# Moving 256 rows of an MLP's second weight to 40 partitions and five DMA engines

## The chip, the cores and the metric

The kernel runs on one core of a Trainium2 chip. The metric is the device time of one execution in microseconds, the median of several runs. The core has a tensor engine (PE, with a separate weight load, PEld), a vector engine (DVE), a scalar engine (ACT), a general engine (POOL), a sync engine (SP) that here only issues loads, and sixteen DMA engines that carry all of them.

## The reference

One decode step of a transformer block for two tokens (batch 2, one position each), width 576. The input is normalised, and an attention branch and an MLP branch are both added to it:

```python
xn = layernorm(x)                                   # x: 2 x 1 x 576
out = x + A(xn, k_cache, v_cache, wq, wo) + B(xn, w1, b1, w2, b2)

# A: 32 query heads over 16 key/value heads, last 2048 of 8192 positions
q = xn @ wq                                         # wq: 576 x 4096
p = softmax((q . k[:, :, 8192 - 2048:]) * 128 ** -0.5)
A = (p . v[:, :, 8192 - 2048:]) @ wo                # wo: 4096 x 576

# B: squared ReLU
h = max(xn @ w1 + b1, 0) ** 2                       # w1: 576 x 4608
B = h @ w2 + b2                                     # w2: 4608 x 576
```

All tensors are bfloat16. Nearly all of the work is reading: the page counts 53.62 MB read, of which the keys and values are 33.6 MB, and each of w1 and w2 5.3 MB.

## The kernel before, in words

**Attention.** The 32 pairs of batch and key/value head are done in NU = 8 units of four heads (`TH`). A unit's keys are one tile of 128 partitions x 8192 elements (16 KB per partition, 2 MB), its values another. `load_k` and `load_v` (L341 to L347) issue them from SP into a pool of six equal buffers, `kvpool`. `step(u)` (L363) transposes the keys of unit u on TensorE in eight groups (`transposes`, L232), multiplies them with the queries (`scores`, L245), and in between multiplies the values of unit u - 2 with their probabilities (`pv`, L281). `softmax` (L255) runs on DVE, POOL and ACT. After every second unit `wo_proj` (L297) projects four heads of both tokens onto the output.

**MLP.** `mlp_h_block(c)` (L316) multiplies the c-th block of 128 rows of w1 (the fifth block has the remaining 64) with the input and adds to a PSUM tile `hT_ps`; its output is transposed, with the hidden unit on the partition. The 4608 hidden units are cut into two halves of L1 = 2304 (S = 2), each half into FR = 18 columns: hidden unit s*2304 + p*18 + r sits on partition p in column s*18 + r. So there are NFC = 36 columns of 128 units, and 36 matmuls for each of five blocks. With the last block DVE adds b1 and squares (L327 to L333). `mlp_o` (L335) multiplies a column of h with the matching row of w2: for partition p and column r that is row s*2304 + p*18 + r, so a w2 tile has on partition p a run of consecutive rows of w2, r0 to r1, of 1152 bytes each. `issue_w2` (L126) loads such a piece into a buffer of the same pool as keys and values. The list of the pieces is

```python
W2P = [(0, 0, 9), (0, 9, 18), (1, 0, 9), (1, 9, 15), (1, 15, 18)]
```

that is, half, first row, end row: nine rows, nine, nine, six and three.

**Output.** `out_acc` (L211) does two matmuls of 288 columns for every row, the two halves of the width side by side in one PSUM tile `out_ps`. Everything adds to that tile: x itself and b2 at the start, the four projections of the attention, and the w2 rows. At the end DVE copies it (L414) and SP and ACT store a half each.

**Order.** The tile framework places each engine's instructions: it takes program order as priority and lets a later instruction go ahead when an earlier one isn't ready by its own reckoning. Waits and buffers are put in by it. In the profile SP issues in program order: queries' weights and the first keys, w1 between the first units, then values, wo and keys of the following units, and behind the last values (L407) the w2 pieces, each as soon as a buffer is free. POOL issues the two bias loads at the start (L146, L148).

Of the kernel before, what the change touches and what calls it, by code (L numbers as in the profile page):

```python
# [9 lines left out]
BF16 = mybir.dt.bfloat16  # L10
# [6 lines left out]
def kernel(  # L17
# [14 lines left out]
    nc = tc.nc  # L32
    P = 128
    B, Sq, D = A_x.shape
    _, Hkv, Sk, Dh = A_k_cache.shape
    Hq = A_wq.shape[1] // Dh
    F = B_w1.shape[1]
# [11 lines left out]
    NU = NQ * B  # L49
# [6 lines left out]
    S = P // REM  # L56
    KC = NFULL + 1
    NXN = NFULL + S
    LQ = (Hq * Dh) // S
    L1 = F // S  # L60
    FR = L1 // P
    NFC = S * FR
    OH = D // 2
    WR = NC * Dh // P
    DW = Dh // WR
# [2 lines left out]
    const = ctx.enter_context(tc.tile_pool(name="const", bufs=1))  # L68
# [12 lines left out]
    k_tiles, v_tiles, wq_tiles, w1_tiles, wo_tiles, w2_tiles = {}, {}, {}, {}, {}, {}  # L81
# [7 lines left out]
    def issue_kv(tiles, cache, u, name, parts=1):  # L89
        tl = kvpool.tile([P, UE], BF16, tag="kv", name=f"{name}_{u}")  # L90
        v = unit_view(cache, u)
        n = UE // parts
        tiles[u] = tl
        return [lambda i=i: nc.sync.dma_start(out=tl[:, i * n:(i + 1) * n], in_=v[:, :, i * n:(i + 1) * n])  # L94
                for i in range(parts)]
# [10 lines left out]
    def issue_wq(c):  # L106
        issue_w(wq_tiles, A_wq, c, "wq", Hq * Dh, LQ)
# [1 line left out]
    def issue_w1(c):  # L109
        issue_w(w1_tiles, B_w1, c, "w1", F, L1)  # L110

    def w_operands(tiles, c, col0, L, step=1):
        last = col0 + (P - 1) * step
        if c < NFULL:
            return tiles[c][:, col0:last + 1:step], c
        sg = col0 // L
        assert last // L == sg
        return tiles[c][:, col0 - sg * L:last - sg * L + 1:step], NFULL + sg

    def issue_wo(tq):  # L120
        tl = wopool.tile([P, WR, D], BF16, tag="wo_sb", name=f"wo_{tq}")
        n = NC * Dh
        nc.sync.dma_start(out=tl[:], in_=A_wo[tq * n:(tq + 1) * n, :].rearrange("(p r) n -> p r n", r=WR))
        wo_tiles[tq] = tl

    def issue_w2(s, r0, r1):  # L126
        tl = kvpool.tile([P, (r1 - r0) * D], BF16, tag="kv", name=f"w2_{s}_{r0}")
        rows = B_w2[s * L1:(s + 1) * L1, :].rearrange("(p r) n -> p (r n)", r=FR)
        nc.sync.dma_start(out=tl[:], in_=rows[:, r0 * D:r1 * D])
        w2_tiles[(s, r0)] = tl  # L130

    x_sb = const.tile([B, D], BF16, name="x_sb")
    nc.scalar.dma_start(out=x_sb[:], in_=x2d)
# [8 lines left out]
    k0[1]()  # L142
    for c in range(2, KC):
        issue_wq(c)
    b1_sb = const.tile([P, S, FR], BF16, name="b1_sb")
    nc.gpsimd.dma_start(out=b1_sb[:], in_=B_b1.rearrange("(s p r) -> p s r", s=S, p=P))  # L146
    b2_sb = const.tile([1, D], BF16, name="b2_sb")
    nc.gpsimd.dma_start(out=b2_sb[:], in_=B_b2.rearrange("(o n) -> o n", o=1))  # L148

# [39 lines left out]
    xnT = const.tile([P, NXN, B], BF16, name="xnT")  # L189
# [21 lines left out]
    def out_acc(lhsT, rhs_of, start=False, stop=False):  # L211
        for i in range(2):
            nc.tensor.matmul(out_ps[32 * i:32 * i + B, :], lhsT=lhsT, rhs=rhs_of(i * OH, (i + 1) * OH),  # L213
                             start=start, stop=stop, skip_group_check=True)
# [7 lines left out]
    def q_block(c):  # L222
        for h in range(Hq):
            lhsT, xc = w_operands(wq_tiles, c, h * Dh, LQ)
            nc.tensor.matmul(qT_ps[:, h, :], lhsT=lhsT, rhs=xnT[:, xc, :],  # L225
                             start=(c == 0 and h == 0), stop=(c == KC - 1), skip_group_check=True)
        if c == KC - 1:
            nc.vector.tensor_copy(out=qT_all[:].rearrange("p b h -> p h b"), in_=qT_ps[:])
# [52 lines left out]
    def pv(u, g):  # L281
        tq, b = divmod(u, B)
        if g == 0:
            oT_cur[u] = psum.tile([P, NC], F32, tag="misc", bufs=2, name=f"oT_ps_{u}")
        oT_ps = oT_cur[u]
        v_sb = v_tiles[u]
        for i in range(JG):
            j = g * JG + i
            nc.tensor.matmul(oT_ps[:], lhsT=v_sb[:, j * Dh:(j + 1) * Dh], rhs=pT_tiles[u][:, j, :],  # L289
                             start=(j == 0), stop=(j == NJ - 1))  # L290
        if g == NG - 1:
            if b == 0:
                oG_tiles[tq] = keep.tile([P, NC, B], BF16, tag="oG", name=f"oG_{tq}")
            nc.vector.tensor_tensor(out=oG_tiles[tq][:, :, b], in0=oT_ps[:], in1=rinv_tiles.pop(u)[:], op=ALU.mult)
            pT_tiles.pop(u)

    def wo_proj(tq):  # L297
        oG = oG_tiles.pop(tq)
        rr = work.tile([P, WR, NC * B], BF16, tag="rr", name=f"rr_{tq}")
        nc.vector.tensor_tensor(  # L300
            out=rr[:],
            in0=oG[:].rearrange("p h b -> p (h b)").unsqueeze(1).to_broadcast([P, WR, NC * B]),
            in1=rmask[:].unsqueeze(2).to_broadcast([P, WR, NC * B]), op=ALU.mult)
        wps = psum.tile([P, WR, B], F32, tag="misc", bufs=2, name=f"wps_{tq}")
        for h in range(NC):
            nc.tensor.matmul(wps[:], lhsT=sel[:, h, :, :].rearrange("p a c -> p (a c)"),
                             rhs=rr[:, :, h * B:(h + 1) * B], start=(h == 0), stop=(h == NC - 1))
        ws = work.tile([P, WR, B], BF16, tag="ws", name=f"ws_{tq}")
        nc.vector.tensor_copy(out=ws[:], in_=wps[:])  # L309
        wo_sb = wo_tiles.pop(tq)  # L310
        for r in range(WR):
            out_acc(ws[:, r, :], lambda a, z: wo_sb[:, r, a:z])

    mlp = {}

    def mlp_h_block(c):  # L316
        if c == 0:
            mlp["ps"] = psum.tile([P, NFC, B], F32, tag="misc", bufs=2, name="hT_ps")
        hT_ps = mlp["ps"]
        for s in range(S):  # L320
            for r in range(FR):
                lhsT, xc = w_operands(w1_tiles, c, s * L1 + r, L1, FR)
                nc.tensor.matmul(hT_ps[:, s * FR + r, :], lhsT=lhsT, rhs=xnT[:, xc, :],  # L323
                                 start=(c == 0 and s == 0 and r == 0), stop=(c == KC - 1), skip_group_check=True)
        if c == KC - 1:
            t1 = work.tile([P, NFC, B], F32, tag="t1", name="t1")
            nc.vector.tensor_tensor(out=t1[:], in0=hT_ps[:],  # L327
                                    in1=b1_sb[:].rearrange("p s r -> p (s r)").unsqueeze(2).to_broadcast([P, NFC, B]),
                                    op=ALU.add)
            hT_sb = const.tile([P, NFC, B], BF16, name="hT_sb")  # L330
            nc.vector.scalar_tensor_tensor(out=hT_sb[:], in0=t1[:], scalar=0.0, in1=t1[:],
                                           op0=ALU.max, op1=ALU.mult)
            mlp["h"] = hT_sb  # L333

    def mlp_o(s, r0, r1, last=False):  # L335
        w2_sb = w2_tiles.pop((s, r0))
        for r in range(r0, r1):
            o = (r - r0) * D
            out_acc(mlp["h"][:, s * FR + r, :], lambda a, z: w2_sb[:, o + a:o + z], stop=(last and r == r1 - 1))

    def load_k(u):  # L341
        for f in issue_kv(k_tiles, A_k_cache, u, "k"):
            f()

    def load_v(u):
        for f in issue_kv(v_tiles, A_v_cache, u, "v"):
            f()  # L347

    W2P = [(0, 0, 9), (0, 9, 18), (1, 0, 9), (1, 9, 15), (1, 15, 18)]

    load_k(1)
    issue_w1(0)
    issue_w1(1)
    load_v(0)
    load_k(2)
    for c in range(2, KC):
        issue_w1(c)
    load_v(1)
    issue_wo(0)
    load_k(3)  # L360
    nxt = {0: [], 1: [], 2: [lambda: load_v(2), lambda: load_k(4)]}

    def step(u, extra=()):  # L363
        for g in range(NG + 2):
            if g < NG:
                transposes(u, g)
            if u >= 1 and 1 <= g <= NG:
                if u >= 2:
                    pv(u - 2, g - 1)
            if g >= 2:  # L370
                scores(u, g - 2)
        softmax(u)
# [15 lines left out]
    for u in range(2, NU + 2):  # L388
        if u < NU:
            step(u)  # L390
        else:
            for g in range(NG):
                pv(u - 2, g)
        if u == 2:
            for c in range(2, KC):
                mlp_h_block(c)
        if u - 2 >= 1 and (u - 2) % B == B - 1:
            wo_proj((u - 2) // B)
        if u < NU:
            load_v(u)  # L400
            if u % B == 0:
                issue_wo(u // B)
            if u + 2 < NU:
                load_k(u + 2)
        if u >= NU - 1:
            pass
        if u == NU - 1:  # L407
            for w in W2P:
                issue_w2(*w)
    for i, w in enumerate(W2P):  # L410
        mlp_o(*w, last=(i == len(W2P) - 1))

# [34 lines left out]
```

## Time and profile before

| what | us |
|---|---|
| median of 3 runs | 137.40 (137.31 to 137.52) |
| the profiled execution's own time | 137.42 |
| its span, first to last instruction | 135.6 |
| PE busy | 102.5 (76%) |
| DVE busy | 53.9 (40%) |
| ACT busy | 43.0 (32%) |
| POOL busy | 10.0 (7%) |
| mean granted TensorE clock | 0.759 of full |
| moved by DMA | 53.90 MB, mean 397 GB/s |

The page of the profile gives, over the span, each engine's busy time, a row of forty slices with the busy share in tenths, the DMA queues with packets and bytes (q1 is SP's, q10 ACT's, q0 POOL's, q8 and q14 carry instructions), and the chain of work that ended last, followed back from the end. A line such as "start, length, PE out_ps L213 x6" is six matmuls of line 213 that write the tile out_ps. A query for stretches of time gives the engines' busy time, the granted TensorE clock and the mean busy share of the sixteen DMA engines in each. Behind these views lie the records of single DMA packets (queue, start, length, size, not the engine) and of the times at which a load's up to sixteen parts reported their landing.

### The profile page before, as it was taken

The numbers are of one execution on the slowest core, as the hardware profiler recorded it, in microseconds if no ns is written. First come the engines' busy times: TensorE is split into PE (matmuls) and PEld (weight loads), VectorE is DVE, ScalarE is ACT, GpSimd is POOL, SyncE is SP. The second block draws the span as 40 slices with busy tenths as digits, with TensorE's granted clock in tenths as the row PEclk, the third lists the DMA queues.
The fourth block names the chain that finished last, engine by engine and source line by source line (L and its number), as shares of the span: only waits on it lengthen the run. The fifth ranks groups of instructions, "written<-read, shape, count | busy, mean of one in ns | idle before, by whom it ended". The sixth has DMA issues, their size and how long they took to land.

```text
span 135.6 us, 4461 instructions
## 1 busy us (share of the span) xinstructions
PE 102.5 (76%) x2054; PEld 91.9 (68%) x2054; DVE 53.9 (40%) x124; ACT 43.0 (32%) x47; POOL 10.0 (7%) x31
## 2 busy tenths in 40 slices
PE   1049947599968999879943993999399599768961
PEld 0039947589968999839933993688399479664530
DVE  7502421574352325422653446355634645660001
ACT  6705550165012521004701550272155127110000
POOL 6400000110110001100011001101100110110000
PEclk9999985569855685556985698698559959955599
DMA  5999999999999999999999999999999999999940
GB/s 112 418 419 418 428 442 402 420 429 440 430 393 430 438 411 409 444 425 396 440 440 406 445 420 425 404 443 423 425 430 413 430 415 426 422 410 417 393 166 1
DMA packets 5278, 53.90 MB, mean 397 GB/s; under 512 B 630, under 2 KB 652, under 8 KB 1164
## 3 DMA queue, kind: packets, MB, share of 16 engines
q1 hardware_dynamic: 5188, 53.61, 94.7%
q8 instruction: 16, 0.26, 0.8%
q0 software_dynamic: 64, 0.01, 0.0%
q14 instruction: 2, 0.02, 0.0%
q10 hardware_dynamic: 8, 0.00, 0.0%
HBM read 53.62 MB, written 0.00 MB: 395 GB/s over the span
## 4 chain that ended last, share of the span: by engine, by line
DMA 55%; PE 35%; DVE 3%; issue 2%; POOL 1%; ACT 1%; SPq 1%; POOLq 0%; ACTq 0%
DMA k<-in_A_k_cache_dram 41%; PE kT_ps L237 18%; DMA w<-in_B_w_dram 10%; PE hT_ps L323 5%; DMA b_sb<-in_B_b_dram 4%; PE sc_ps L252 4%; PE out_ps L213 4%; PE oT_ps L289 3%; PE qT_ps L225 1%; ACT kT L240 1%; POOL b_sb L146 1%; DVE l L271 1%; DVE sub L266 1%; SPq L94 0%; DVE fin_sb L414 0%
## 5 line engine op out<-in xcount | busy, mean ns | idle before, releaser
L237 PE MATMUL kT_ps<-ident,k 128*128 128x128 bf16 x512 | 47.3, 260 | 9.9 <-DMA k<-in_A_k_cache_dram 9.9
L237 PEld LDWEIGHTS <-k 128*128 128x128 bf16 x512 | 39.6, 119 | 11.8 <-DMA k<-in_A_k_cache_dram 10.7
L240 ACT COPY kT<-kT_ps 128x1024 bf16<-128x1024 bf16 x32 | 32.3, 1012 | 40.1 <-PE kT_ps L237 40.0
L242 DVE COPY kT<-kT_ps 128x1024 bf16<-128x1024 bf16 x32 | 22.0, 690 | 33.4 <-PE kT_ps L237 33.4
L252 PE MATMUL sc_ps<-qT_all,kT 128*128 128x8 bf16 x512 | 21.6, 168 | 1.6 <-ACT kT L240 0.8
L252 PEld LDWEIGHTS <-kT 128*128 128x128 bf16 x512 | 19.1, 100 | 2.6 <-ACT kT L240 1.2
L289 PE MATMUL oT_ps<-pT,v 128*128 128x8 bf16 x512 | 15.5, 167 | 1.9 <-issue 1.4
L269 ACT ACTIVATE pT<-sub 128x512 bf16<-128x512 f32 x8 | 5.0, 630 | 35.1 <-DVE sub L266 35.1
L289 PEld LDWEIGHTS <-v 128*128 128x128 bf16 x512 | 14.4, 99 | 2.1 <-issue 1.6
L271 DVE TENSOR_REDUCE l<-pT 128x8 f32<-128x512 bf16 x8 | 8.5, 1066 | 4.2 <-ACT pT L269 4.2
L213 PE MATMUL out_ps<-wo,ws 128*2 128x288 bf16 x64 | 8.3, 438 | 2.4 <-DVE ws L309 2.4
L323 PE MATMUL hT_ps<-xnT,w 128*128 128x2 bf16 x144 | 9.8, 201 | 0.0
L323 PEld LDWEIGHTS <-w 128*128 128x128 bf16 x144 | 9.4, 165 | 0.0
L258 DVE TENSOR_REDUCE m<-sc_ps 128x8 f32<-128x512 f32 x8 | 5.5, 692 | 9.7 <-PE sc_ps L252 9.7
L262 POOL PARTITION_ALL_REDUCE gmax<-m x8 | 2.9, 364 | 84.8 <-DVE m L260 84.8
L213 PE MATMUL out_ps<-w,hT_sb 128*2 128x288 bf16 x72 | 6.9, 353 | 1.3 <-DMA w<-in_B_w_dram 1.3
L213 PEld LDWEIGHTS <-ws 128*2 128x2 bf16 x64 | 3.5, 115 | 5.4 <-DVE ws L309 2.8
L213 PEld LDWEIGHTS <-hT_sb 128*2 128x2 bf16 x72 | 3.8, 103 | 4.3 <-issue 1.9
L266 DVE TENSOR_TENSOR sub<-sc_ps,gm 128x512 f32<-128x512 f32 x8 | 5.5, 692 | 0.3
L225 PE MATMUL qT_ps<-xnT,wq 128*128 128x2 bf16 x128 | 4.0, 165 | 2.2 <-DMA wq<-in_A_wq_dram 1.9
L225 PEld LDWEIGHTS <-wq 128*128 128x128 bf16 x128 | 3.9, 103 | 2.2 <-DMA wq<-in_A_wq_dram 2.0
L273 POOL PARTITION_ALL_REDUCE lsum<-l x8 | 3.2, 398 | 24.5 <-DVE l L271 24.5
(58 smaller groups left out, 35.1 us busy)
## 6 DMA issues: line engine op xcount, KB each, us to landing
v<-in_A_v_cache_dram SPq DMA_DIRECT2D x8, 2048.0 KB, 28.4
k<-in_A_k_cache_dram SPq DMA_DIRECT2D x7, 2048.0 KB, 29.4
w<-in_B_w_dram SPq DMA_DIRECT2D x4, 1152.0 KB, 17.7
wo<-in_A_wo_dram SPq DMA_DIRECT2D x4, 1152.0 KB, 27.4
wq<-in_A_wq_dram SPq DMA_DIRECT2D x4, 1024.0 KB, 6.9
w<-in_B_w_dram SPq DMA_DIRECT2D x3, 1296.0 KB, 22.7
k<-in_A_k_cache_dram SPq DMA_DIRECT2D x2, 1024.0 KB, 9.1
w<-in_B_w_dram SPq DMA_DIRECT2D x1, 864.0 KB, 15.7
```

What stands on the lines that cost most here:

```text
L213: nc.tensor.matmul(out_ps[32 * i:32 * i + B, :], lhsT=lhsT, rhs=rhs_of(i * OH, (i + 1) * OH), start=start, stop=stop, skip_group_check=True)
L225: nc.tensor.matmul(qT_ps[:, h, :], lhsT=lhsT, rhs=xnT[:, xc, :], start=(c == 0 and h == 0), stop=(c == KC - 1), skip_group_check=True)
L237: nc.tensor.transpose(out=kT_ps[:, i * P:(i + 1) * P], in_=k_sb[:, j * Dh:(j + 1) * Dh], identity=ident[:])
L240: nc.scalar.copy(out=kT[:], in_=kT_ps[:])
L242: nc.vector.tensor_copy(out=kT[:], in_=kT_ps[:])
L252: nc.tensor.matmul(sc_ps[:, g * JG + i, :], lhsT=kT[:, i * P:(i + 1) * P], rhs=qT_all[:, b, tq * NC:(tq + 1) * NC], start=True, stop=True)
L258: nc.vector.tensor_reduce(out=m1[:], in_=sc_ps[:].rearrange("p j c -> p c j"), axis=AX.X, op=ALU.max)
L266: nc.vector.tensor_tensor(out=sub[:], in0=sc_ps[:], in1=gm2[:].unsqueeze(1).to_broadcast([P, NJ, NC]), op=ALU.subtract)
L269: nc.scalar.activation(out=pT[:], in_=sub[:], func=ACT.Exp, scale=scale)
L271: nc.vector.tensor_reduce(out=l1[:], in_=pT[:].rearrange("p j c -> p c j"), axis=AX.X, op=ALU.add)
L289: nc.tensor.matmul(oT_ps[:], lhsT=v_sb[:, j * Dh:(j + 1) * Dh], rhs=pT_tiles[u][:, j, :], start=(j == 0), stop=(j == NJ - 1))
L323: nc.tensor.matmul(hT_ps[:, s * FR + r, :], lhsT=lhsT, rhs=xnT[:, xc, :], start=(c == 0 and s == 0 and r == 0), stop=(c == KC - 1), skip_g ...
```

## The change

256 of the 4608 rows of w2, the last ones, leave the 128-partition pieces. The second half keeps FT = 16 columns of 128 units (2048 units) in place of 18. Of the other 256 units 240 are laid on 40 partitions with six columns (XR = 6, XP = 40), so partition p holds six consecutive rows of w2, and the last 16 on 16 partitions with one column. The 240 rows are loaded by eight DMAs of five partitions each (partitions i, i+8, i+16, i+24 and i+32), one behind each of `load_v(1)`, `load_k(3)`, `load_v(2)`, `load_k(4)` and so on; the 16 rows follow the eighth. They have tiles of their own. `mlp_x`, new, does their seven columns after `pv` of unit 6. There are now 41 columns in h; `hT_ps` is set to zero by DVE first, and b1 by POOL, since some columns don't fill all partitions; b1 comes in four loads in place of one. The w2 pieces become nine, nine, nine, four, two and one rows. Two unused statements go.

```diff
+    XR, XP = 6, 40
+    FT = (L1 - XR * XP) // P
+    FX = L1 - FT * P
+    XQ = FX - XR * XP
+    FX0 = L1 + FT * P
+    CH = [(r, FR, P) for r in range(FR)] + [(L1 + r, FT, P) for r in range(FT)]
+    CH += [(FX0 + r, XR, XP) for r in range(XR)] + [(FX0 + XR * XP, 1, XQ)]
+    NFC = len(CH)
...
     def issue_w2(s, r0, r1):
+        nr = FT if s else FR
...
+        rows = B_w2[s * L1:s * L1 + nr * P, :].rearrange("(p r) n -> p (r n)", r=nr)
...
+    x_parts = list(range(8))
+
+    def issue_w2x():
+        if x_parts:
+            i = x_parts.pop(0)
+            rows = B_w2[FX0:FX0 + XR * XP, :].rearrange("(e i r) n -> i e (r n)", i=8, r=XR)
+            nc.sync.dma_start(out=w2x_sb[i:XP - 8 + i + 1:8, :], in_=rows[i])
+            if not x_parts:
+                nc.sync.dma_start(out=w2y_sb[:], in_=B_w2[FX0 + XR * XP:F, :])
...
-    b1_sb = const.tile([P, S, FR], BF16, name="b1_sb")
-    nc.gpsimd.dma_start(out=b1_sb[:], in_=B_b1.rearrange("(s p r) -> p s r", s=S, p=P))
+    b1_sb = const.tile([P, NFC], BF16, name="b1_sb")
+    nc.gpsimd.memset(b1_sb[:], 0.0)
+    o = 0
+    for f0, n, m in ((0, FR, P), (L1, FT, P), (FX0, XR, XP), (FX0 + XR * XP, 1, XQ)):
+        nc.gpsimd.dma_start(out=b1_sb[0:m, o:o + n], in_=B_b1[f0:f0 + n * m].rearrange("(p r) -> p r", r=n))
+        o += n
...
             mlp["ps"] = psum.tile([P, NFC, B], F32, tag="misc", bufs=2, name="hT_ps")
+            nc.vector.memset(mlp["ps"][:], 0.0)
...
+        for i, (f0, step, m) in enumerate(CH):
+            lhsT, xc = w_operands(w1_tiles, c, f0, L1, step, m)
+            nc.tensor.matmul(hT_ps[0:m, i, :], lhsT=lhsT, rhs=xnT[:, xc, :],
+                             start=(c == 0 and i == 0), stop=(c == KC - 1), skip_group_check=True)
...
+    def mlp_x():
+        for i, (f0, step, m) in enumerate(CH[FR + FT:]):
+            w = w2x_sb[0:m, i * D:(i + 1) * D] if m == XP else w2y_sb[:]
+            out_acc(mlp["h"][0:m, FR + FT + i, :], lambda a, z: w[:, a:z])
...
     def load_k(u):
...
+        if u >= 3:
+            issue_w2x()
...
     def load_v(u):
...
+        if u >= 1:
+            issue_w2x()
...
-    W2P = [(0, 0, 9), (0, 9, 18), (1, 0, 9), (1, 9, 15), (1, 15, 18)]
+    W2P = [(0, 0, 9), (0, 9, 18), (1, 0, 9), (1, 9, 13), (1, 13, 15), (1, 15, 16)]
...
+        if u == NU:
+            mlp_x()
```

More of the change, by code (lines that the diff above doesn't have):

```diff
@@ L61 @@
     FR = L1 // P
-    NFC = S * FR
+    XR, XP = 6, 40
[6 more added lines that the diff above has]
+    NFC = len(CH)
     OH = D // 2
@@ L110, in issue_w1, with w_operands @@
         issue_w(w1_tiles, B_w1, c, "w1", F, L1)
-    def w_operands(tiles, c, col0, L, step=1):
-        last = col0 + (P - 1) * step
+    def w_operands(tiles, c, col0, L, step=1, m=P):
+        last = col0 + (m - 1) * step
         if c < NFULL:
@@ L126, in issue_w2 @@
     def issue_w2(s, r0, r1):
+        nr = FT if s else FR
         tl = kvpool.tile([P, (r1 - r0) * D], BF16, tag="kv", name=f"w2_{s}_{r0}")
-        rows = B_w2[s * L1:(s + 1) * L1, :].rearrange("(p r) n -> p (r n)", r=FR)
+        rows = B_w2[s * L1:s * L1 + nr * P, :].rearrange("(p r) n -> p (r n)", r=nr)
         nc.sync.dma_start(out=tl[:], in_=rows[:, r0 * D:r1 * D])
         w2_tiles[(s, r0)] = tl
+    w2x_sb = const.tile([P, XR * D], BF16, name="w2x_sb")
+    w2y_sb = const.tile([XQ, D], BF16, name="w2y_sb")
+    x_parts = list(range(8))
[6 more added lines that the diff above has]
+                nc.sync.dma_start(out=w2y_sb[:], in_=B_w2[FX0 + XR * XP:F, :])
     x_sb = const.tile([B, D], BF16, name="x_sb")
@@ L318, in mlp_h_block @@
             mlp["ps"] = psum.tile([P, NFC, B], F32, tag="misc", bufs=2, name="hT_ps")
+            nc.vector.memset(mlp["ps"][:], 0.0)
         hT_ps = mlp["ps"]
[L320 to L324, printed above, removed]
+        for i, (f0, step, m) in enumerate(CH):
+            lhsT, xc = w_operands(w1_tiles, c, f0, L1, step, m)
+            nc.tensor.matmul(hT_ps[0:m, i, :], lhsT=lhsT, rhs=xnT[:, xc, :],
+                             start=(c == 0 and i == 0), stop=(c == KC - 1), skip_group_check=True)
         if c == KC - 1:
@@ L327, in mlp_h_block @@
             nc.vector.tensor_tensor(out=t1[:], in0=hT_ps[:],
-                                    in1=b1_sb[:].rearrange("p s r -> p (s r)").unsqueeze(2).to_broadcast([P, NFC, B]),
+                                    in1=b1_sb[:].unsqueeze(2).to_broadcast([P, NFC, B]),
                                     op=ALU.add)
@@ L360 @@
     load_k(3)
-    nxt = {0: [], 1: [], 2: [lambda: load_v(2), lambda: load_k(4)]}
     def step(u, extra=()):
@@ L404 @@
                 load_k(u + 2)
-        if u >= NU - 1:
-            pass
+        if u == NU:
+            mlp_x()
         if u == NU - 1:
```

## The prediction

> **What bounds the kernel now.** I read the page's summary first, then the chain that ended last, then the stretches of the last 14 us, and last the records of single DMA packets. The page:
>
> ```profile
> span 135.6 us, 4461 instructions
> DMA  5999999999999999999999999999999999999940
> q1 hardware_dynamic: 5188, 53.61, 94.7%
> q8 instruction: 16, 0.26, 0.8%
> ```
>
> The DMA engines are at 9 tenths from the second slice to the 38th; the loads (q1) fill 94.7% of sixteen engines' span. No other engine is above 76%. So time is bytes, and what follows the last byte. The end of the chain (start, length, what) shows the second part:
>
> ```profile
> 119.21 13.05 DMA w<-in_B_w_dram
> 132.26 0.04 issue
> 132.30 0.55 PE out_ps L213 x6
> 132.85 0.02 issue
> 132.87 0.45 DVE fin_sb L414
> ```
>
> The last piece of w2 lands at 132.26, its six matmuls (three rows, two halves each) take 0.55, then comes the copy-out. Now the stretches (PE, PEld, DVE, ACT, POOL busy; then granted clock, DMA share, GB/s):
>
> ```profile
> 118.14:121.55 3.41, 2.21 (x71) 2.08 (x72) 2.25 (x5) 0.63 (x1) 0.40 (x1) 0.50 1.01 421
> 121.55:124.97 3.42, 2.51 (x29) 1.41 (x29) 0.64 (x3) 0.00 (x0) 0.00 (x0) 0.50 0.99 405
> 124.97:128.38 3.41, 3.41 (x32) 1.86 (x30) 0.00 (x0) 0.00 (x0) 0.00 (x0) 0.50 0.99 409
> 128.38:129.20 0.82, 0.54 (x10) 0.26 (x8) 0.00 (x0) 0.00 (x0) 0.00 (x0) 1.00 0.69 279
> 129.20:131.20 2.00, 1.23 (x18) 0.75 (x18) 0.00 (x0) 0.00 (x0) 0.00 (x0) 1.00 0.50 191
> 131.20:132.30 1.10, 0.90 (x12) 0.52 (x12) 0.00 (x0) 0.00 (x0) 0.00 (x0) 1.00 0.22 85
> ```
>
> The share drops from 0.99 to exactly 0.50 and stays there for 2 us: eight engines have finished, eight still carry. The landing records of the last piece say the same: eight arrive at 128.90 to 129.88, eight at 132.11 to 132.26. A gap of 2.2 to 3.3 us is being wasted on half of the engines. Its source is the q8 row: 16 instruction packets of 16 KB. Where one goes, the engine loses time: one runs 79.61 to 80.67, and that engine's next data packet takes 1.115 us instead of 0.612, so 2.157 - 0.612 = 1.55 us are lost. Followed from packet end to packet start, the 16 hit eight engines in a fixed rotation, twice each: 2 x 1.55 = 3.1 us, which is the gap.
>
> [...] No load of before has five; x_sb and the two output stores have two partitions and show two packets each[...]. [...] here the window 124.97 to 128.38 is 3.41 busy of 3.41 and the clock goes from 0.50 to 1.00 at its end.
>
> **The change, part by part.**
>
> *Bytes at the end.* Before, the fourth and fifth piece (6 and 3 rows, packets of 6912 and 3456 B) land at 131.19 and 132.26 after the third's 129.12: 2.07 + 1.07 = 3.14. After, the pieces are 4, 2 and 1 rows, eight packets each: 4608 B at 0.177 (the 4608 B packets of w1's rest), 2304 B at about 0.093 (estimate, between these rows), 1152 B at about 0.05 (x_sb's two took 0.048 and 0.069). 8 x (0.177 + 0.093 + 0.05) = 2.56, plus one 1152 B packet per engine for the last 16 rows, 0.05: 2.61. Gain on every engine 0.53.
>
> *The eight five-partition loads.* Each puts one 6912 B packet on each of five engines; 2.07 / 8 = 0.259 each, so 8 x 0.259 = 2.07 us more there. If those five are of the early eight, their latest landing goes from at most 129.88 to 129.88 + 2.07 - 0.53 = 131.42, still before the late eight's 132.26 - 0.53 = 131.73, and costs nothing. If one is of the late eight, the last landing is 131.73 + 2.07 = 133.80. Which holds is the main question, taken up below.
>
> *SP's queue.* Nine issues more (v1, k3, v2, k4, v3, k5, v4, k6 each get one behind them), at most 0.54 each (the row for 128 partitions), 4.9 in all, behind waits for buffers that take over 80 us; the tiles are their own, so no new buffer wait. k and v land 28 to 29 us after issue at the median, five times a 2 MB load's 5 us, so a late issue doesn't empty the DMA queues. The sixth w2 piece needs one more of the six kv buffers; the fifth got its at 119.21 when pv(6) ended, the sixth gets its when pv(7) ends, 121.4 to 123.2, over 7 us before its turn.
>
> *TensorE, middle.* mlp_h goes from 36 to 41 matmuls in each of five blocks: 25 x 0.062 (72 took 4.48 in the chain) = 1.56 us, around 33 to 55. Plus a new wait: the first hT matmul waits for a DVE memset of hT_ps (nearest row: out_ps's, 0.30). If the DVE has that memset behind softmax(1), the wait lasts to 40.28 at worst, 7.5 us after 32.7; queued behind it on TensorE are scores, step 2's transposes, and for those kv buffers SP. Cover: TensorE idles 1.86 us at 39.42, 1.12 at 57.24 and 4.26 at 69.17 waiting for k; and the 23 us of loads in flight cover SP. I take 0; without cover up to 9.
>
> *Start.* b1 becomes a POOL memset and four POOL loads ahead of b2. b1's issue took 1.02, b2's 0.56; three more at 0.56 to 1.02 plus about 0.1 is 1.8 to 3.2 us later for b2, for which TensorE waits until 8.33 (5.0 idle). The sel memset and copies on POOL follow; first used at 58.36. Cover: TensorE idles 1.91 at 17.84 and 1.51 at 24.40 for loads; SP's w1 issues at 10.25 and 14.5 go behind loads that land up to 24.4. I take 0; without cover 3.
>
> *TensorE, end.* mlp_x's seven rows come after pv(6) and before pv(7). A row (two matmuls side by side) takes 0.240 at clock 0.50, 0.122 at 1.00: 0.86 to 1.68. The idle 0.51 ahead of pv(7) hides part, so wo's projection and the w2 rows start d = 0.35 to 1.17 late; I take 1.1. At 124.70 + 1.1 the w2 rows start; until the clock's release at 128.38 10.8 rows run, the remaining 23.2 of 34 need 2.8: 131.2, before 131.73. So it is hidden behind the landing, barely.
>
> *After the last byte.* One row instead of three: 0.55 - 2 x 0.122 = 0.31.
>
> *Sum.* The landing 0.53 earlier, the tail 0.24: 0.77. The profiled execution took 137.42 for a span of 135.6; 137.42 - 0.77 = 136.65. The median of the runs shown is 137.40, so no correction.
>
> **Rivals.**
>
> *A, the forecast: engines 0 to 4 are early ones.* For: I can follow five engines surely that never get an instruction packet; in the order in which engines begin the first load they are the 4th, 6th, 7th, 8th and 16th. Sure late ones are the 13th and 14th. The other nine share six late places and can't be told apart, as their packets end within 2 ns. If starts go up with the number (the two packets of x_sb start 23 ns apart, those of the stores 22), then four of five sure early ones lie in the lower half, and the simplest set of eight is: upper half late. Against: the order has a jitter of its own, 16th is early, and of the first five to start, one or two must be late if it is taken literally. 136.65; with d used up fully or 6912 B packets at 0.30, 137.0; at best (the tail's small packets for nothing) 136.4.
>
> *B: at least one of the five is late.* Landing 133.80, tail 0.04 + 0.29 instead of 0.04 + 0.57 to the copy: the end comes 133.80 - 132.26 - 0.24 = 1.30 later, 138.7. This is the slower one; it decides as soon as one of five engines finishes later than 131.73 - 2.07 + 0.53 = 130.2 in the trace of before. If the late one has only part of its delay by then, 138.0 to 138.9.
>
> *C: TensorE becomes the end.* [...] of wo's 8 rows and w2's 34, begun at 124.5, 28 run slow and 14 fast, ending at about 133.0 against 132.85: no gain, 137.2 to 137.5. For: slack left in A is 0.5. [...]
>
> *D: the start or the memset isn't covered.* Then up to 3 us; against it stand the 28 us of loads in flight and 9.9 us of TensorE idle for k.
>
> **How the numbers follow.** A 0.58, C 0.07, B 0.30, D 0.05. About 0.2% (0.3 us) is what a measurement here can tell from no change. Faster: A, 0.58. Same: C, 0.07. Slower: B and D, 0.35. A's own range is 136.35 to 137.05; to leave out at most 2 in 10 the range must take in B: 136.35 to 138.8. The predicted time is A's.
>
> **What would show it.** A right: the DMA share falls later and more steeply (less than 1 us at 0.50 near the end), the last piece's landings spread less than 1 us, the last landing near 131.7, two matmuls after it, a chain that ends in w2's load. B: a share below 0.4 for about 2 us at the end, since only the loaded late engines still carry. C: the chain's end is TensorE's L213 without a wait. Start: the wait for b_sb longer than 5.0, with no k load later than before by 70 us. The forecast is wrong first of all if engine numbers are not what the start order suggests, then if a 17th instruction packet falls before the end[...].

## The result, and the profile after

The kernel after takes 144.18 us at the median of four runs (142.08 to 144.4) against 137.43 before: a ratio of 1.041, 95% interval 1.029 to 1.054. Two of the four (144.28 and 144.40) lie over 1.5% above the fastest, count as slow and are left out of the ratio. Six later runs of it gave 142.67 (141.68 to 143.48), a ratio of 1.037 (1.033 to 1.040); below, a time set against after's is set against this one. The forecast was 136.65, in a range of 136.35 to 138.8. The change makes the kernel slower by 5 to 6 us.

The profile is that of the run of 144.28. That of a later run of 143.27 has the same waits for rr (8.5 us in all) and also ends in TensorE.

The page of the kernel after, the lines that answer to those shown of before:

```profile
span 142.5 us, 4549 instructions
DMA  3999999999999999999999999999999999998100
q1 hardware_dynamic: 5444, 53.61, 90.8%
q8 instruction: 16, 0.26, 0.8%
```

The loads move the same 53.61 MB, and there are still sixteen instruction packets. But the row of the DMA engines now ends in "8100" where it ended in "9940": for two slices (7 us) at the end nearly nothing is carried. The bound has changed. The end of the chain (start, length, what), from the two projections on:

```profile
112.48 0.17 DVE rr L324
112.69 0.38 PE wps L330 x8
...
117.26 2.67 PE kT_ps L261 x24
...
130.46 0.30 DVE rr L324
...
130.81 0.38 PE wps L330 x8
...
131.44 7.34 PE out_ps L237 x43
...
138.80 0.45 DVE fin_sb L445
```

Before, one entry of 13 us, a load of w2, stood ahead of the last matmuls. Now no load is in the last part at all: it is DVE's rr, TensorE's projection, and 7.34 us of TensorE alone. The stretches of the end (PE, PEld, DVE, ACT, POOL busy; granted clock, DMA share, GB/s) say the same:

```profile
122.45:128.28 5.83, 4.05 (x125) 3.81 (x123) 3.18 (x8) 2.36 (x3) 0.37 (x1) 1.00 1.00 426
128.28:130.12 1.84, 1.82 (x64) 1.76 (x64) 1.24 (x2) 0.00 (x0) 0.40 (x1) 0.63 0.91 371
130.12:133.31 3.19, 2.24 (x24) 1.24 (x25) 0.67 (x4) 0.00 (x0) 0.00 (x0) 0.50 0.67 245
133.31:138.80 5.49, 5.45 (x70) 3.19 (x66) 0.00 (x0) 0.00 (x0) 0.00 (x0) 0.79 0.00 0
```

From 133.31 on, where TensorE begins w2's rows, the DMA share is 0.00: the last piece of w2 had landed at 133.44. So two things happened. TensorE comes to w2's rows 8.6 us later than before (133.31 against 124.70), and, hidden behind that, the last landing is 1.2 us later (133.44 against 132.26) where the forecast had it 0.53 earlier.

TensorE's delay can be read off its starts. The key transposes of unit 6 begin at 99.27 (before 97.31): 1.96 late, since the keys land later. Those of unit 7, the last, begin at 117.20 (before 109.80): 5.4 more. The waits of TensorE say which; of after:

```profile
PE wps L330 <- DVE rr L324: 8.5, 4, 3.5
PE kT_ps L261 <- DMA k<-in_A_k_cache_dram: 6.9, 6, 3.2
```

and of before (total, times, longest):

```profile
PE wps L306 <- DVE rr L300: 2.9, 4, 1.1
PE kT_ps L237 <- DMA k<-in_A_k_cache_dram: 9.9, 4, 4.3
```

The wait for rr, DVE's preparation of the projection, rose from 2.9 to 8.5. The time lines show why (start, length, engine, line, operation, in brackets the idle time before). Before, around the third projection:

```profile
105.16 0.77 PE L289 MATMUL oT_ps<-pT,v 128*128 128x8 bf16 x25
105.34 0.69 DVE L258 TENSOR_REDUCE m<-sc_ps 128x8 f32<-128x512 f32 x1 [0.87 <-PE sc_ps L252]
105.97 0.17 DVE L294 TENSOR_TENSOR oG<-oT_ps,rinv 128x8 bf16<-128x8 f32 x1
...
106.17 0.29 DVE L300 TENSOR_TENSOR rr<-oG,rmask 128x128 bf16<-128x128 bf16 x1
...
106.52 0.35 PE L306 MATMUL wps<-rr,sel 128*128 128x16 bf16 x8 [0.59 <-DVE rr L300]
```

and after:

```profile
107.40 1.79 PE L313 MATMUL oT_ps<-pT,v 128*128 128x8 bf16 x64
107.58 0.69 DVE L282 TENSOR_REDUCE m<-sc_ps 128x8 f32<-128x512 f32 x1 [0.45 <-PE sc_ps L276]
...
110.63 1.05 DVE L295 TENSOR_REDUCE l<-pT 128x8 f32<-128x512 bf16 x1 [0.69 <-ACT pT L293]
111.60 0.16 DVE L318 TENSOR_TENSOR oG<-oT_ps,rinv 128x8 bf16<-128x8 f32 x1
...
112.40 0.24 DVE L324 TENSOR_TENSOR rr<-oG,rmask 128x128 bf16<-128x128 bf16 x1
112.69 0.36 PE L330 MATMUL wps<-rr,sel 128*128 128x16 bf16 x8 [3.50 <-DVE rr L324]
```

Before, pv ran in pieces between the scores (the x25 is its last), and oG (pv's output, normalised) and rr stood right behind it, inside the softmax of the unit that follows. After, pv is one block of 64 behind all scores, and oG and rr stand behind almost that whole softmax, POOL's and ACT's parts included. TensorE has the projection next in its order and sits idle for 3.50 us, and the same 3.53 one projection earlier. In this stretch, from unit 6's keys to unit 7's, 1.3 us are lost up to the end of pv, where the same 192 matmuls run at a granted clock of 0.67 in place of 0.78 (in the later profile it is 0.5 us). 2.2 us come from the waits (3.50 against 0.59 for rr, less 0.7 that the wait for the next copy became shorter), and 1.85 from mlp_x, which stands from 115.34 to 117.20 ahead of the last keys' transposes. No line that the diff changes has to do with pv, oG or rr.

### The profile page after: what moved, and what is told of

It is laid out like the page before. It is cut to its first block, busy times and chain, and to the rows that moved or that the text cites. A ratio compares the mean times of both kernels' runs of the same rounds, so it can differ in the third digit from the quotient of the medians.

```text
span 142.5 us, 4549 instructions
## 1 busy us (share of the span) xinstructions
PE 107.0 (75%) x2089; PEld 95.4 (67%) x2089; DVE 53.9 (38%) x125; ACT 43.0 (30%) x47; POOL 11.7 (8%) x35
## 3 DMA queue, kind: packets, MB, share of 16 engines
q1 hardware_dynamic: 5444, 53.61, 90.8%
## 4 chain that ended last, share of the span: by engine, by line
DMA 66%; PE 18%; DVE 5%; SPq 3%; ACT 2%; issue 1%; POOL 1%; POOLq 0%; ACTq 0%; DVEq 0%
DMA k<-in_A_k_cache_dram 46%; DMA v<-in_A_v_cache_dram 19%; PE out_ps L237 8%; PE kT_ps L261 8%; PE sc_ps L276 2%; SPq L107 2%; DVE l L295 1%; ACT kT L264 1%; DVE m L282 1%; DVE sub L290 1%; ACT pT L293 1%; SPq L101 1%; POOL gmax L286 1%; PE wps L330 1%; DVE rr L324 0%
## 5 line engine op out<-in xcount | busy, mean ns | idle before, releaser
L261 PE MATMUL kT_ps<-ident,k 128*128 128x128 bf16 x512 | 48.0, 261 | 7.1 <-DMA k<-in_A_k_cache_dram 6.9
L313 PE MATMUL oT_ps<-pT,v 128*128 128x8 bf16 x512 | 14.5, 167 | 2.2 <-ACT pT L293 1.5
L313 PEld LDWEIGHTS <-v 128*128 128x128 bf16 x512 | 13.9, 99 | 2.4 <-issue 2.4
L347 PE MATMUL hT_ps<-xnT,w 128*128 128x2 bf16 (+2 forms) x164 | 11.4, 200 | 0.0
L347 PEld LDWEIGHTS <-w 128*128 128x128 bf16 (+2 forms) x164 | 10.9, 159 | 0.1
L330 PE MATMUL wps<-rr,sel 128*128 128x16 bf16 x32 | 1.5, 175 | 8.5 <-DVE rr L324 8.5
L330 PEld LDWEIGHTS <-sel 128*128 128x128 bf16 x32 | 1.4, 104 | 8.7 <-issue 7.9
L237 PEld LDWEIGHTS <-hT_sb 128*2 128x2 bf16 (+2 forms) x82 | 4.0, 99 | 3.6 <-issue 1.0
```

The lines of the kernel that those rows point to most:

```text
L261: nc.tensor.transpose(out=kT_ps[:, i * P:(i + 1) * P], in_=k_sb[:, j * Dh:(j + 1) * Dh], identity=ident[:])
L347: nc.tensor.matmul(hT_ps[0:m, i, :], lhsT=lhsT, rhs=xnT[:, xc, :], start=(c == 0 and i == 0), stop=(c == KC - 1), skip_group_check=True)
```

## The experiments

Theory 1: the nine small loads do it, in two ways: by where they stand in SP's queue, which shifts the order of TensorE and DVE, and by making the DMA engines' other packets slower. Theory 2: the computation's edits do it. Theory 3: rival B, a late engine among the five.

**The loads alone, from SP (e1_loads_only).** The kernel before, with the nine loads into tiles that nothing reads:

```diff
     def load_k(u):
...
+        if u >= 3:
+            issue_w2x()      # nc.sync, five partitions i, i+8, ... as after
     def load_v(u):
...
+        if u >= 1:
+            issue_w2x()
```

> The kernel before plus the nine small w2 loads of the kernel after, at their places in SP's queue, into tiles that nothing reads; every w2 row is still also loaded as before, 0.29 MB more in all. Theory 1 (the loads do it, by their place in SP's queue, which shifts pv behind the scores and rr behind the next softmax, and by slowing the DMA engines): 141 to 143, DVE's rr wait over 3 us twice. Theory 2 (the computation's edits do it: 41 columns, mlp_x ahead of the last keys, the memset): at most 138, rr wait as before. Theory 3 (a late engine among the five, nothing else): 139 to 139.6, w2's last landing 2 us later, rr wait as before.

Measured: 141.74 (140.93 to 142.54), ratio 1.032 (1.026 to 1.037), with the rr wait of after:

```profile
PE wps L318 <- DVE rr L312: 8.9, 4, 3.5
```

Nine loads that nobody waits for cost 4.3 us. Theory 2 falls for the larger part of the loss.

**The same loads from ACT's queue (e1_scalar).**

```diff
-            nc.sync.dma_start(out=w2x_sb[i:40 - 8 + i + 1:8, :], in_=rows[i])
+            nc.scalar.dma_start(out=w2x_sb[i:40 - 8 + i + 1:8, :], in_=rows[i])
```

> The same added loads, issued from ACT's queue and not from SP's, so that SP's queue and the order of TensorE and DVE stay as before. What is left of the loss is the DMA engines' own. Theory 1: 138.5 to 139.7 (five engines 2.07 us later, the other eleven about 1 us), rr wait as before. Theory 2: at most 138. Theory 3: 139 to 139.6, the same as with SP.

Measured: 139.75 (139.70 to 139.79), ratio 1.017 (1.016 to 1.019), and

```profile
PE wps L318 <- DVE rr L312: 3.0, 4, 1.1
```

The order is that of before, and 2.0 of the 4.3 us are gone. (From ACT the small packets also run earlier, at 9 to 32 us; from SP it was 51 to 98.) The other 2.35 are the DMA engines' own. The keys of unit 6 land 2.1 us later than before (99.38 against 97.26) and the last w2 piece 2.0 later (134.24 against 132.26). TensorE, late through the keys, ends the chain 1.0 us behind that landing:

```profile
127.88 7.41 PE out_ps L225 x84
```

The time is 0.05 us above the range of theory 1 and 0.15 above that of theory 3. By time alone theory 3 would do for this rest, but not by the landings of the last w2 piece. Before, eight engines landed at 128.90 to 129.88; here none lands ahead of 131.01, and at most five of those eight carry small packets, if the five are the same for all eight loads, as the landings of e6_scalar_ports below suggest. So engines without one are late too.

**The order alone (e9_order).** The kernel before, no load changed, the order of after held by hand:

```diff
+            with after(sc_last, u + 1, 2 <= u <= 5 and j == 0):
                 nc.tensor.matmul(oT_ps[:], ...)              # pv behind all scores
+            with after(l1_ins, u + 1, 2 <= u <= 5):
                 nc.vector.tensor_tensor(out=oG_tiles[tq][:, :, b], ...)
+        with after(rinv_ins, 2 * tq + 2, 1 <= tq <= 2):
             nc.vector.tensor_tensor(out=rr[:], ...)
```

> The kernel before with no load changed, only the order of TensorE and DVE held as it is after: pv of units 2 to 5 behind all scores, the normalisation of pv's output behind the next softmax's sums, rr of the second and third projection behind the next softmax's reciprocal. Theory 1: slower by 1 to 4 us (138.4 to 141.4), rr wait over 3 us twice, and the end no longer w2's landing if it is over 2. Theories 2 and 3: within 0.5 us of before.

Measured: 140.31 (138.88 to 140.99), ratio 1.017 (1.010 to 1.025), and the wait is there:

```profile
PE wps L313 <- DVE rr L307: 8.9, 4, 3.5
```

So the order by itself costs 2.4 us (by the ratio) to 2.9 (by the medians), with every load as before. Theories 2 and 3 expected nothing.

**One load in place of eight (e2_two_loads).** The kernel after, with

```diff
-            i = x_parts.pop(0)
-            rows = B_w2[FX0:FX0 + XR * XP, :].rearrange("(e i r) n -> i e (r n)", i=8, r=XR)
-            nc.sync.dma_start(out=w2x_sb[i:XP - 8 + i + 1:8, :], in_=rows[i])
+            x_parts.clear()
+            rows = B_w2[FX0:FX0 + XR * XP, :].rearrange("(p r) n -> p (r n)", r=XR)
+            nc.sync.dma_start(out=w2x_sb[0:XP, :], in_=rows)
```

> The kernel after with its 240 rows in one load of forty partitions behind the first value load, followed by the 16 rows, in place of eight five-partition loads at eight places; columns, mlp_x, memsets, pieces of the tail as after. Eight engines then carry it, and early, and the order of pv and rr is as before. Theory 1: 138 to 139.5, what is left being mlp_x ahead of the last keys and eight engines' 1.3 us more. Theory 2: 143 or more, as after. Theory 3: 136.5 to 138 if the eight engines aren't late, else 138.5.

Measured: 139.81 (139.40 to 140.59), 0.3 above the range of theory 1, and 2.9 less than after. The longest rr wait is 0.8: with two issues in place of nine the order is that of before. That eight engines carry the load was the author's estimate; ten parts of it report their landing (52.70 to 55.75), so it was ten. Its last landing is at 133.83 and its matmuls end at 134.19, so both the engines and TensorE are late here.

**Other partitions for the same loads (e6_scalar_ports).** Why should a load on five engines slow the other eleven? What can still be varied is where the loads write. In e1_scalar the five partitions of a load lie 8 apart: i, i+8, i+16, i+24 and i+32. That others would be cheaper was the author's estimate; no earlier run shows it. I moved them 4 apart, to (i mod 4) + 32*(i div 4) + 0, 4, 8, 12 and 16, from ACT's queue:

```diff
-            nc.scalar.dma_start(out=w2x_sb[i:40 - 8 + i + 1:8, :], in_=rows[i])
+            nc.scalar.dma_start(out=w2x_sb[(i % 4) + 32 * (i // 4):(i % 4) + 32 * (i // 4) + 17:4, :], in_=rows[i])
```

> As e1_scalar (the kernel before plus the nine small loads from ACT's queue, into tiles that nothing reads), with only the destination partitions changed: load i goes to partitions (i mod 4) + 32*(i div 4) + 0, 4, 8, 12, 16 in place of i + 0, 8, 16, 24, 32, [...] the packets of all other engines keep their length, the eleven engines without a small packet land as before, the five 2.07 later and still before 132.3: 137.3 to 138.0. Fixed-cost theory (each load costs every engine about 0.2 us, wherever it writes): as e1_scalar, 139.5 to 139.9. Late-engine theory (one of the five lands last in the kernel before): 139.0 to 139.6, one to five engines alone 2 us later at the end.

Measured: 137.74 (137.60 to 138.65), ratio 1.0024 (1.0008 to 1.0041), against 139.75 with the other partitions. Both pages have a row of the rate in 40 slices of 3.4 us; of e1_scalar:

```profile
GB/s 117 421 401 389 423 375 389 350 439 395 400 425 408 435 418 417 438 416 423 409 441 413 437 418 432 414 427 412 430 427 423 418 410 435 436 400 427 404 219 1
```

and of e6_scalar_ports:

```profile
GB/s 124 413 412 425 422 431 415 414 434 424 405 418 407 434 425 414 433 420 418 414 442 415 434 420 425 414 427 425 425 420 434 413 412 444 410 419 419 413 249 1
```

The small packets run between 9 and 32 us, the third to the tenth slice. In the sixth to the eighth the first kernel has 375, 389 and 350, the second 431, 415 and 414. In the packet records from 5 to 40 us, the time over the median of their size comes to 2.18 us per engine in e1_scalar, 0.39 in e6_scalar_ports and 0.24 before. What differs is the destination's partitions alone, and ACT issues nine loads in both, so its issues aren't the cost either. That the partitions cost 2 us is shown (139.75 against 137.74); why those 8 apart cost it and those 4 apart don't is not.

The landings of the last piece settle theory 3 as well. In e6_scalar_ports three engines land at 129.20 to 129.51, the other thirteen at 131.39 to 132.58. Before it was eight at 128.90 to 129.88 and eight at 132.11 to 132.26. If a loaded engine were one of the late eight, it would land at 134.2 or later (132.11 + 2.07); none does. In order of time, three of the early eight are 0.3 to 0.5 later, the late ones 0.2 to 0.3, and five are 2.3 to 2.6 later: the five loaded engines were early ones.

**The kernel after, loads from ACT (e8_scalar).** All else as after:

```diff
-            nc.sync.dma_start(out=w2x_sb[i:XP - 8 + i + 1:8, :], in_=rows[i])
+            nc.scalar.dma_start(out=w2x_sb[i:XP - 8 + i + 1:8, :], in_=rows[i])
...
-                nc.sync.dma_start(out=w2y_sb[:], in_=B_w2[FX0 + XR * XP:F, :])
+                nc.scalar.dma_start(out=w2y_sb[:], in_=B_w2[FX0 + XR * XP:F, :])
```

> The kernel after with the nine small loads issued from ACT's queue in place of SP's, all else as after. The order of TensorE and DVE is then that of before[...]. Theory 1[...]: 139.5 to 141.5, that is, 2.5 to 4.5 less than after, rr wait 1 us or less. Theory 2 (the computation's edits cost most of it): 143 or more.

Measured: 139.94 (139.78 to 140.94), rr wait 0.8 at the longest. One word in two lines brings back 2.7 us.

**mlp_x at another place (e4_x_last).**

```diff
         if u == NU:
-            mlp_x()
...
     for i, w in enumerate(W2P):
         mlp_o(*w, last=(i == len(W2P) - 1))
+        if i == 1:
+            mlp_x()          # behind the second w2 piece
```

> The kernel after with the fourteen matmuls of mlp_x moved from ahead of the last keys' transposes to behind the second w2 piece; nothing else. They stand on TensorE's way to the end in both places, so only what the later place hides is gained: the last keys' transposes start up to 1.85 us earlier, the w2 rows end 0.9 to 1.7 us later than that. Theory 1: 143.0 to 144.2. If mlp_x's place is what costs most: 142.3 or less.

Measured: 141.98 (141.73 to 144.16). By the words of the expectation, 142.3 or less, mlp_x's place would be what costs most. But these figures were set against after's first four runs; against 142.67 the gain is 0.7, a small part of the loss.

**The tail alone (e5_tail).** The kernel before with

```diff
-    W2P = [(0, 0, 9), (0, 9, 18), (1, 0, 9), (1, 9, 15), (1, 15, 18)]
+    W2P = [(0, 0, 9), (0, 9, 18), (1, 0, 9), (1, 9, 15), (1, 15, 17), (1, 17, 18)]
```

> The kernel before with the last two w2 pieces of 6 and 3 rows cut into 6, 2 and 1, nothing else. One row's matmuls after the last byte in place of three: 0.31 less, for 0.07 more of packets: 137.1 to 137.3. If TensorE or the waits for buffers set the end rather than the last landing: 137.4 to 137.6.

Measured: 137.16, ratio 0.9987 (0.9973 to 1.0000): 0.28 less by the medians, and in the range. The expectation takes 0.31 for what is saved; that is what two matmuls leave behind the landing, and 0.24 is saved. In its profile (a run of 137.29) 0.33 us pass from the landing to TensorE's end in place of 0.57, but the landing itself is 0.21 later. It is the one kernel here whose median is below before's.

**All three causes taken away, and one at a time.** In e12_ports_act the kernel after has its loads on partitions 4 apart and on ACT's queue; mlp_x stays. e10_ports_act_early also moves mlp_x behind the first projection and issues two small loads at each place in place of one; e15_pool_memset is e10 with its one extra memset on POOL, and e11_ports_sp has the partitions 4 apart and the loads on SP. The 240 rows now lie on two groups of 20 partitions, so each block of mlp_h has 47 matmuls:

```diff
+    CH += [(FX0 + g * XG * XR + r, XR, XG, 32 * g, FR + FT + r) for g in range(2) for r in range(XR)]
...
-            nc.sync.dma_start(out=w2x_sb[i:XP - 8 + i + 1:8, :], in_=rows[i])
+            nc.scalar.dma_start(out=w2x_sb[32 * g + j:32 * g + j + 17:4, :], in_=rows[j])   # e11: nc.sync
...
+    nc.vector.memset(w2x_sb[0:32, :], 0.0)          # e15: on POOL
...
-        if u == NU:
+        if u == 3:                                  # e10 and e15 only
             mlp_x()
```

> The kernel after with all three suspected costs taken away: [...] (partitions 0 to 19 and 32 to 51, the same 240 rows, five engines, eight loads; each of the five blocks of mlp_h gets six matmuls more, 47, for the two groups of 20 partitions), they are issued from ACT's queue, and mlp_x stands behind the first wo projection, ahead of the fourth unit's keys, where TensorE waits for a load later. [...] 136.6 to 137.1 (before's 137.44 less 0.53 of landing and 0.24 of tail, plus the 0.3 that the loads still cost in e6_scalar_ports). If something of the change that is left (47 columns, memsets, small b1 loads, the finer tail) costs more than 0.5: 137.5 or more.

> As e10_ports_act_early, but mlp_x stays where it is after, ahead of the last keys' transposes, and each place issues one small load. If mlp_x's place costs what it takes there, 1.85, and TensorE is then the end: 137.1 to 138.3. If it is hidden, as the prediction had it: as e10_ports_act_early within 0.2.

> The kernel after[...] (partitions 0 to 19 and 32 to 51, 47 matmuls in each block); SP issues the loads and the order of TensorE and DVE is that of after. Theory: [...]the order's and mlp_x's remain: 140 to 142, rr wait over 3 us twice. If the order only hurt through late loads: 138.5 or less.

> As e10_ports_act_early, with the memset of the small loads' tile on POOL in place of DVE, where it held TensorE's first matmuls back by about 3 us. If that late start is why e10_ports_act_early was slower than expected: 136.7 to 137.3. If TensorE's 55 added matmuls and the clock make it the end: 137.5 to 139.3, as there.

Measured: e12_ports_act 137.99 (137.74 to 138.69), e10_ports_act_early 139.14 (137.53 to 141.26; ratio 1.0095, 1.0062 to 1.0127), e15_pool_memset 138.14 (137.06 to 138.84), e11_ports_sp 143.37 (142.38 to 144.29).

e12_ports_act lies in its first range, where TensorE is the end with mlp_x on its way. It is 1.95 less than e8_scalar, which differs in the partitions (and has 30 matmuls and a memset less): the same 2 us as on the kernel before.

e10_ports_act_early and e15_pool_memset both miss the range in which nothing is left to lose, and fall in the other, 137.5 or more. Moving mlp_x early brought nothing that can be seen. Why e10 is the slowest of the three isn't shown. TensorE waits 5.9 us for the memset at the start in place of 3.0, but e12 has that wait too; and the one profile of e10 is of its fastest run, 137.53, which ends with w2's landing.

e11_ports_sp lies 1.4 above its range. It differs from e12_ports_act in the queue of the small loads alone, has the order of after, and takes 5.4 us more. The waits for rr in e12 and in e11:

```profile
PE wps L333 <- DVE rr L327: 2.6, 4, 0.8
PE wps L333 <- DVE rr L327: 8.5, 4, 3.5
```

So with the partitions 4 apart, nine loads on SP's queue cost as much, by the order, as the whole change did. In e11_ports_sp the transposes of unit 6 start at 98.00 in place of 100.09 in the later profile of after, but those of unit 7 at 116.96 in place of 117.20: once the order makes TensorE wait for DVE, keys that come 2 us earlier are worth 0.2.

The end of the chain in e12_ports_act:

```profile
125.33 6.85 PE out_ps L240 x43
132.17 0.02 issue
132.19 0.45 DVE fin_sb L448
```

Its last landing is at 131.74, and the forecast's step said 131.73. TensorE ends at 132.15, 0.4 behind it. The copy starts 0.68 us earlier than before. And yet the time, 137.74 in this run and 137.99 at the median, is 0.3 to 0.6 longer: from the copy's end to the span's end are 2.67 us (before 2.30), and the time around the span is 2.23 to 2.44 in its runs (before 1.75 to 1.93).

**Half the change, with none of the costs (e14_half).** 120 rows on 20 partitions, in four loads with the partitions 4 apart, from ACT:

```diff
-    XR, XP = 6, 40
+    XR, XP = 6, 20
...
-            nc.sync.dma_start(out=w2x_sb[i:XP - 8 + i + 1:8, :], in_=rows[i])
+            nc.scalar.dma_start(out=w2x_sb[i:XP - 4 + i + 1:4, :], in_=rows[i])
...
+    W2P = [(0, 0, 9), (0, 9, 18), (1, 0, 9), (1, 9, 14), (1, 14, 16), (1, 16, 17)]
```

with mlp_x behind the first projection.

> The change at half size without the three costs: 120 rows of w2 on the 20 partitions 0 to 19, four loads of five partitions[...], issued from ACT's queue, 8 rows behind them; 42 columns, mlp_x behind the first wo projection; half two keeps 17 columns, its pieces 5, 2 and 1 rows at the end. If the step of moving bytes to engines with time left is sound: the last landing 0.1 to 0.2 earlier, one row after it in place of three, 136.9 to 137.2. If what is left of the edits (columns, memsets, small b1 loads, mlp_x) costs more than it brings: 137.5 or more.

Measured: 137.55 (137.13 to 137.93), ratio 1.0008 (0.9998 to 1.0018): no gain. But its span is 135.1 to 135.3 in all but one of fourteen runs, where before's is 135.4 to 135.7: the 0.4 expected are there. They go where the profile doesn't look: the time less the span is 2.01 to 2.07 in six of the runs and 2.42 to 2.58 in eight, against 1.76 to 1.92 of before beside them. Its landings are three at 128.52 to 128.98, five at 129.69 to 130.64 and eight at 131.50 to 132.00: the three groups that the forecast's engines ask for. So the step of the forecast shows in the span, and what ate it lies outside. What that is stays open; no run varied it.

**The kernel after once more (after_again)**, beside these four:

> The kernel after, unchanged, for more of its times beside those of these runs: 142 to 144.4, as seen. It tells nothing apart; e4_x_last and e11_ports_sp are read against it.

142.67, as given above. These six times go with the granted clock: 141.68 and 141.83 at 0.791, 142.59 to 143.27 at 0.768 and 0.769, 143.48 at 0.734. In e1_scalar, which also ends in TensorE, they don't: 139.70 to 139.79 at 0.752 to 0.827.

The sum, from medians:

| kernel | order of after | partitions 8 apart | columns, mlp_x, tail | us |
|---|---|---|---|---|
| before | no | no loads | no | 137.4 |
| e6_scalar_ports | no | no | no | 137.74 |
| e1_scalar | no | yes | no | 139.75 |
| e9_order | yes | no loads | no | 140.31 |
| e1_loads_only | yes | yes | no | 141.74 |
| e12_ports_act | no | no | yes | 137.99 |
| e8_scalar | no | yes | yes | 139.94 |
| e11_ports_sp | yes | no | yes | 143.37 |
| after | yes | yes | yes | 142.67 |

The partitions cost 2.0 (139.75 - 137.74) and 1.95 (139.94 - 137.99), and less where the order holds TensorE back: 1.4 (141.74 - 140.31), and nothing that is seen between e11_ports_sp and after. The order costs 2.0 (141.74 - 139.75), 2.4 to 2.9 (e9_order), 2.7 (142.67 - 139.94) and, with the partitions 4 apart, 5.4 (143.37 - 137.99). All the computation's edits together cost 0.2 (139.94 - 139.75) to 0.9 (142.67 - 141.74). So the costs don't add: one hides behind another, and how large a share looks depends on what was taken away before it. With the computation's edits in place, the order adds as much as the whole loss; the partitions without it add 2 us.

**Behind the copy and around the span.** One part of the loss is neither. I took the time of each profiled execution and left out of it the stretch from the span's start to the end of DVE's last copy. In all kernels with the computation of before (before, e1_loads_only, e1_scalar, e6_scalar_ports, e9_order, e5_tail) 4.0 to 4.1 us remain. In all kernels with the changed computation it is 4.4 (e14_half) to 5.1 (e12_ports_act), and 5.0 in both profiles of after. So up to 1.0 us is lost there, more than the 0.77 that the forecast had to win. A part of it can be seen in the span: before, SP finishes its closing waits 0.2 us after its store has landed; in e12_ports_act it waits for the store first, and the waits behind that take 0.6 us. Which edit brings this about, no run tells.

## Why the prediction was wrong

**"The eight five-partition loads" is the step that was mis-sized.** It charged each load to its own five engines, 2.07 us, and found them hidden there. In "the forecast: engines 0 to 4 are early ones" it was right that the five are early ones, as three, five and eight landings show; that they are numbers 0 to 4 was the author's estimate, since no record names an engine. But the loads also cost all sixteen engines about 2 us, by the partitions that they write: 2.0 at the last landing of e1_scalar, where they lie 8 apart, 0.3 with 4 apart (e6_scalar_ports). Nothing in the trace of before shows a small load, and I bounded its cost only by the packets' own length.

**"SP's queue" is the step that failed.** It looked at buffers and at loads in flight, and put nine more issues at nothing (at most 0.54 each; the eight took 0.72 to 0.85 in after). It asked how late SP would be, not what the nine issues do to the order in which the framework places TensorE's and DVE's instructions. They moved pv behind the scores and rr behind a softmax: 2.0 to 5.4 us, by what else is in the kernel. The same loads from ACT leave the order alone. By which of its reckonings the framework does so, no run tells.

**"TensorE, end".** mlp_x doesn't stand between pv(6) and pv(7) but ahead of the last keys' transposes, and takes 1.85 us, not 0.35 to 1.17. On its own this would have cost the forecast little: e12_ports_act has it there, and TensorE ends 0.4 after the landing in the profiled run.

**"Bytes at the end" and "After the last byte"** held: a last landing of 131.74 for 131.73 (e12_ports_act), 0.28 for the finer tail (e5_tail, 0.24 forecast). That the landing agrees to 0.01 is luck, since the same loads with partitions 4 apart moved it by 0.3 in e6_scalar_ports, where the step had nothing. **"Start"** cost nothing, as forecast, but not by the cover: the matmul on b_sb starts at 6.93, 1.4 us earlier than before (8.33), where the step had it 1.8 to 3.2 later; the wait for b_sb is 3.3, below 5.0. **"TensorE, middle"**: TensorE waits for keys 6.9 us in place of 9.9 and less idle time is left, but the order and not the 25 matmuls made it the end.

**The rivals.** B has the right sign, and a landing (133.80) between those of the two profiles (133.44 and 134.91), for the wrong reason. C, TensorE becomes the end, is what happened, but was priced at 137.2 to 137.5 with a chance of 0.07, since what would delay TensorE was in no step; that 28 of its rows would run at the slow clock was the author's estimate. The seventeenth instruction packet didn't come (16 in after's q8 row). **Left out of the sum altogether**: what lies behind the copy, taken as unchanged without a reason. With the time around the span it grew by 0.9 us in after (5.0 against 4.1), which by itself would have eaten the forecast's gain.

## What to carry to other kernels

A load on few partitions can cost more than its bytes: here nine of them cost 2.35 us with partitions 8 apart (e1_scalar) and 0.3 with partitions 4 apart (e6_scalar_ports), so try its partitions, and look at the other loads' packets while it runs. Where a framework orders the engines, an issue added to one queue can be an edit to all of them, as the nine issues here were, for 2.0 to 5.4 us; compare the order before putting such an edit at zero, and try the same issue from another queue. When the end passes from a landing to TensorE, earlier landings stop paying: in e11_ports_sp 2 us of them were worth 0.2. And a forecast of less than 1 us has to ask what stands behind the last copy, too.

## What the runs showed of the hardware

Forty packets of 6912 bytes, less than 0.3 MB of 54, put off the last landing by 2.0 us when five engines wrote partitions 8 apart, and by 0.3 when they wrote 4 apart. No gap shows it, as the row of the DMA engines stays at 9 tenths; the packets of other loads get longer. Of those of 16 KB that start from 5 to 40 us, 95 of 337 took over 30 ns more than their usual 613, most of them up to 300. With partitions 4 apart it was 31 of 371, before 1 of 381.

The time around the span isn't the same for all these kernels: it is 1.75 to 1.93 us before, and 2.0 to 2.6 in e14_half, in two groups half a microsecond apart at nearly the same span. A difference of half a microsecond between two kernels can lie wholly outside the profile.
